# A joint-network training step: gelu's k·x·x as one ScalarE square with a scale, in place of a product and a multiplication on VectorE

## The chip, the cores and the metric

The kernel runs on one core of a Trainium2 chip. The metric is the device time of one execution in microseconds (us), as the median of several runs. The engines are named as the profile names them: PE is TensorE (its weight loads are PEld), DVE is VectorE, ACT is ScalarE, POOL is GpSimd, and SP is SyncE, which here only issues transfers. Every engine works through its own queue strictly in order, and waits on semaphores for the others.

## What is computed

The kernel computes a forward pass and all its gradients. Two convolutions of three taps over time, each followed by gelu and by a halving of the time axis, feed a joint network with eight labels `u`:

```python
h = gelu(conv3(x, w1))[:, ::2]            # x: 2 x 16000 x 256, bf16
f = gelu(conv3(h, w2))[:, ::2]            # f: 2 x 4000 x 256
j = tanh((f @ w_f)[:, :, None] + (g @ w_g)[:, None])   # 2 x 4000 x 8 x 256
out = j @ w_o                             # 2 x 4000 x 8 x 256
# returned: out and the gradients of x, w1, w2, g, w_f, w_g, w_o for grad_out
```

Here gelu is the approximate one, which the kernel writes with a sigmoid: with `k = 0.044715` and `a = 2·sqrt(2/pi)`, `gelu(x) = x·s`, where `s = sigmoid(a·x·(1 + k·x·x))`. The backward pass needs gelu's derivative, `s + a·(1 + 3k·x·x)·(1 - s)·gelu(x)`, and so uses `k·x·x` a second time.

## The kernel before

**Tiling.** Channels lie on the 128 partitions, in two halves (`KT = 2`). Time is cut into 16 chunks, eight for each batch entry, of 512 positions of the quarter-rate axis (`CW`, 416 in the last chunk of a batch entry). A tile of gelu is therefore 128 partitions by 2 x 512 = 1024 elements in bf16. Each chunk has three gelus: two after the first convolution (its even and its odd outputs, `conv_units`) and one after the second (`conv2_units`). In chunk 0 each gelu is cut into two halves of 128x512.

**One gelu** (the function `gelu`, helper lines that the profile puts under L194, or L288 in chunk 0's second convolution). ACT has copied the convolution's result from PSUM to `g_x` (L247, L283). The list `first` computes `g_sq = k·x·x` in two DVE instructions (a product, then a multiplication by a constant), then `g_s = (g_sq + 1)·x` on DVE, then the sigmoid on ACT, in place on `g_s`, and then the product `h = s·x` (written to `HT` or `FT`) on DVE. The list `second` is five more DVE instructions, which turn `g_sq`, `g_s` and `h` into the derivative, written to `G1` or `G2`. They go on using `g_sq`.

**The joint stage.** Over the eight labels of a chunk, `tanh` makes `JT` on ACT (L313) from `FE`; `gj` squares it on ACT (`JSQ`, L524), multiplies `grad_out` by `w_o` on PE (L530), and a DVE instruction combines both to `NGZ` (L532). POOL adds the eight `NGZ` up (`ACCN`, `NGFE`, L551). PE computes `out` (L624), which ACT copies out of PSUM to `OUT` (L626), and the gradient of `w_o` (L673), for which `JR`, a transposed `JT`, is fetched by transposing transfers on SP's queue (chunk 0 does it by PE and DVE instead).

**The backward stage** of the chunk before: `d1_units` (PE L337, DVE `GF` L339), `d5_units` (PE L367, DVE `GH` L370), `gwf_units` and `gw2_units` (PE transposes L381, copied out of PSUM at L383 to `rows` by DVE or ACT, then PE L407 and L438), `e_units` (PE L479, which ACT copies to `GX` at L482, and PE L501). Sums over chunks are added into `ACC` tiles by DVE (L323).

**Order.** The function `weave` runs one chunk's joint stage and fills in, at a set ratio, the convolutions of the next chunk and the backward stage of the chunk before. Gelu's instructions are put on a list `later`, from which `pump` takes two at each step. On top of this a scheduler reorders the instructions of each engine when the program is built, so that the queues' final order is its work, and an instruction more or less can move others.

**PSUM.** Seven buffers of the pool `psp` are shared by all these stages. A PE group that needs a buffer waits until DVE or ACT has read an earlier group out of it.

Of the kernel before, what the change touches and what calls it, by code (L numbers as in the profile page):

```python
# [15 lines left out]
ALU = mybir.AluOpType  # L16
ACT = mybir.ActivationFunctionType

GELU_K = 0.044715
GELU_A = float(2.0 * np.sqrt(2.0 / np.pi))  # L20

P = 128
KT = 2
# [8 lines left out]
def kernel(  # L32
# [22 lines left out]
    nc = tc.nc  # L55
# [127 lines left out]
    def scratch(name, spare):  # L183
        if spare:
            return rowp.tile([P, 8, P], BF16, name="rows")[:].rearrange("p (k a) b -> p k (a b)", k=KT)
        return gel.tile([P, KT, CW], BF16, name=name)
# [9 lines left out]
    def gelu(xb, W, h, gp, off, kts=((0, KT),), spare=False):  # L196

        sq, s = scratch("g_sq", spare), scratch("g_s", spare)
        TT, TS, STT = nc.vector.tensor_tensor, nc.vector.tensor_scalar, nc.vector.scalar_tensor_tensor
        first, second = [], []  # L200
        for (k0, k1) in kts:
            sq_, s_, x_ = sq[:, k0:k1, :W], s[:, k0:k1, :W], xb[:, k0:k1, :W]
            h_, gp_ = h[:, k0:k1, off:off + W], gp[:, k0:k1, off:off + W]
            first += [
                partial(TT, out=sq_, in0=x_, in1=x_, op=ALU.mult),
                partial(TS, out=sq_, in0=sq_, scalar1=GELU_K, scalar2=None, op0=ALU.mult),
                partial(STT, out=s_, in0=sq_, scalar=1.0, in1=x_, op0=ALU.add, op1=ALU.mult),
                partial(nc.scalar.activation, out=s_, in_=s_, func=ACT.Sigmoid, scale=GELU_A),
                partial(TT, out=h_, in0=s_, in1=x_, op=ALU.mult),
            ]  # L210
            second += [
                partial(TS, out=sq_, in0=sq_, scalar1=3.0 * GELU_A, scalar2=GELU_A, op0=ALU.mult, op1=ALU.add),
                partial(TS, out=x_, in0=s_, scalar1=-1.0, scalar2=1.0, op0=ALU.mult, op1=ALU.add),
                partial(TT, out=sq_, in0=sq_, in1=x_, op=ALU.mult),
                partial(TT, out=sq_, in0=sq_, in1=h_, op=ALU.mult),
                partial(TT, out=gp_, in0=sq_, in1=s_, op=ALU.add),
            ]
        return first, second
# [6 lines left out]
    def conv_units(n):  # L225
# [11 lines left out]
        for par in range(2):  # L237
            xb = gel.tile([P, KT, CW], BF16, name="g_x")
            for mt in range(KT):
                ps = ps_f32()  # L240
                k = 0
                for (i, c, sh) in taps[par]:
                    for kt in range(KT):
                        nc.tensor.matmul(ps[:, :W], lhsT=W1[:, i, kt, mt * P:(mt + 1) * P],  # L244
                                         rhs=st["X", c][:, kt, 16 + sh:16 + sh + W], start=(k == 0), stop=(k == 5))
                        k += 1
                nc.scalar.copy(out=xb[:, mt, :W], in_=ps[:, :W])  # L247
                yield
            first, second = gelu(xb, W, HT[:, par], G1[:, par], 2, HALVES if n == 0 else ((0, KT),))
            later.extend(first)  # L250
            seconds += second
            if n == 0:
                pump(len(first))
# [11 lines left out]
    def conv2_units(n):  # L265
        b, ci, c0, W = geom(n)
        st = S[n]
        HT = st["HT"]
        if n > 0:
            pump(len(later))  # L270
        FT = ftp.tile([P, KT, CW], BF16, name="FT")
        G2 = ftp.tile([P, KT, CW], BF16, name="G2")
        st["FT"], st["G2"] = FT, G2
        xb = scratch("g_x", n == 0)
        for mt in range(KT):
            ps = ps_f32()
            k = 0
            for (i, par, off) in ((1, 0, 2), (0, 1, 1), (2, 1, 2)):
                for kt in range(KT):
                    nc.tensor.matmul(ps[:, :W], lhsT=W2[:, i, kt, mt * P:(mt + 1) * P],  # L280
                                     rhs=HT[:, par, kt, off:off + W], start=(k == 0), stop=(k == 5))
                    k += 1
            nc.scalar.copy(out=xb[:, mt, :W], in_=ps[:, :W])  # L283
            yield
        first, second = gelu(xb, W, FT, G2, 0, HALVES if n == 0 else ((0, KT),), n == 0)
        if n == 0:
            for f in first:
                f()  # L288
            seconds0[:0] = second
            later.extend(seconds0)  # L290
        else:
            later.extend(first + second)
# [529 lines left out]
    for i in range(KK):  # L822
# [15 lines left out]
                            in_=NGGEc[:].rearrange("p b k u c -> p (b k u) c"),  # L838
# [53 lines left out]
```

## Time and profile before

| what | value |
|---|---|
| median of 3 runs | 883.72 us (882.99 to 883.83) |
| the profiled execution: its own time | 882.75 us |
| the profiled execution: its span | 881.0 us |
| busy share of the span: PE, DVE, ACT, POOL | 95%, 77%, 73%, 48% |
| mean granted PE clock | 0.993 of full speed |
| one full chunk in the steady part | 52.69 us |

The profile is of one execution. A busy PE is not PE at its peak, because the modelled end of a matmul includes its way through the pipeline; matmuls that follow each other without a gap start at shorter distances than they last. "Idle before, and its releaser" is the time that an engine stood still before an instruction, and the last instruction that it waited for. Most of the span is a repetition of chunks; the first 80 us hold the start, in which nothing of a backward stage exists yet, and the last 80 us hold no gelu.

### The profile page before, as it was taken

The numbers are of one execution on the slowest core, as the hardware profiler recorded it, in microseconds if no ns is written. First come the engines' busy times: TensorE is split into PE (matmuls) and PEld (weight loads), VectorE is DVE, ScalarE is ACT, GpSimd is POOL, SyncE is SP. The second block draws the span as 40 slices with busy tenths as digits, with TensorE's granted clock in tenths as the row PEclk, the third lists the DMA queues.
The fourth block names the chain that finished last, engine by engine and source line by source line (L and its number), as shares of the span: only waits on it lengthen the run. The fifth ranks groups of instructions, "written<-read, shape, count | busy, mean of one in ns | idle before, by whom it ended". The sixth has DMA issues, their size and how long they took to land.

```text
span 881.0 us, 17824 instructions
## 1 busy us (share of the span) xinstructions
PE 833.0 (95%) x6574; PEld 600.6 (68%) x6648; DVE 678.9 (77%) x1296; ACT 639.0 (73%) x1016; POOL 419.6 (48%) x457
## 2 busy tenths in 40 slices
PE   7968999999999999998999999999999999999997
PEld 3545676767768577776756668676776757778875
DVE  5998959869596895959789596986959779596553
ACT  2767797686958769595786958768695876958534
POOL 1254544535535455553554544454554535554651
PEclk9998999999999999999999999999999999999999
DMA  9987999999999999999999999999999999997942
GB/s 207 183 182 164 191 229 233 219 210 231 239 227 229 239 179 258 196 227 214 183 197 201 250 219 224 246 230 250 198 227 225 222 237 194 229 209 175 225 136 94
DMA packets 382456, 185.67 MB, mean 211 GB/s; under 512 B 330160, under 2 KB 366280, under 8 KB 382368
## 3 DMA queue, kind: packets, MB, share of 16 engines
q1 hardware_dynamic: 362400, 114.35, 74.3%
q0 software_dynamic: 19968, 70.18, 26.9%
q8 instruction: 52, 0.85, 0.4%
q14 instruction: 36, 0.29, 0.1%
HBM read 54.43 MB, written 50.34 MB: 119 GB/s over the span
## 4 chain that ended last, share of the span: by engine, by line
PE 42%; DVE 29%; ACT 20%; issue 5%; DMA 2%; POOL 0%; ACTq 0%; POOLq 0%; DVEq 0%
DVE g_sq L194 10%; ACT JT L313 8%; PE GWO_ps L673 6%; PE ps L479 5%; PE ps L501 5%; PE ps L624 5%; DVE g_s L194 4%; PE ps L530 4%; PE ps L438 4%; PE ps L280 4%; PE pst L381 3%; DVE NGZ L532 3%; ACT GX L482 3%; DVE GH L370 3%; ACT JSQ L524 3%
## 5 line engine op out<-in xcount | busy, mean ns | idle before, releaser
L551 POOL TENSOR_TENSOR ACCN<-ACCN,NGZ 128x1024 f32<-128x1024 f32 (+1 forms) x80 | 180.3, 2254 | 174.5 <-DVE NGZ L532 173.3
L532 DVE SCALAR_TENSOR_TENSOR NGZ<-JSQ,ps 128x512 bf16<-128x512 bf16 (+1 forms) x256 | 164.2, 668 | 85.6 <-ACT GX L482 40.6
L524 ACT ACTIVATE JSQ<-JT 128x1024 bf16<-128x1024 bf16 (+1 forms) x128 | 135.3, 1059 | 76.2 <-DVE NGZ L532 76.2
L313 ACT ACTIVATE JT<-FE,GE 128x512 bf16<-128x512 f32 (+1 forms) x256 | 171.2, 738 | 0.1
L624 PE MATMUL ps<-WO,JT 128*128 128x256 bf16 x992 | 147.7, 273 | 5.7 <-DVE NGZ L532 4.9
L626 ACT CAST OUT<-ps 128x512 bf16<-128x512 f32 x248 | 143.4, 605 | 5.1 <-PE ps L624 4.7
L530 PE MATMUL ps<-GOT,WOT 128*128 128x512 bf16 (+1 forms) x472 | 134.2, 373 | 9.4 <-DVE GH L370 7.6
L673 PE MATMUL GWO_ps<-GO,JR 128*128 128x256 bf16 x992 | 139.0, 273 | 0.0
L194 ACT ACTIVATE g_s<-g_s 128x1024 bf16<-128x1024 bf16 (+2 forms) x49 | 49.3, 1005 | 98.0 <-DVE g_s L194 98.0
L624 PEld LDWEIGHTS <-JT 128*128 128x128 bf16 x992 | 94.6, 98 | 31.1 <-issue 9.5
L673 PEld LDWEIGHTS <-JR 128*128 128x128 bf16 x992 | 95.0, 98 | 23.8 <-issue 8.5
L323 DVE TENSOR_TENSOR ACC<-ACC,ps 128x512 f32<-128x512 f32 x90 | 59.2, 680 | 59.9 <-PE ps L501 55.3
L479 PE MATMUL ps<-W1T,GH 128*128 128x256 bf16 (+2 forms) x768 | 104.2, 273 | 0.4 <-ACT g_x L283 0.4
L501 PE MATMUL ps<-rows,X 128*128 128x256 bf16 (+2 forms) x768 | 92.3, 273 | 0.0
L244 PE MATMUL ps<-XC,W 128*128 128x512 bf16 (+1 forms) x370 | 88.6, 374 | 0.7 <-DMA XC<-in_x_dram 0.5
L482 ACT CAST GX<-ps 128x512 bf16<-128x512 f32 (+2 forms) x128 | 76.5, 598 | 14.1 <-PE ps L479 7.4
L479 PEld LDWEIGHTS <-GH 128*128 128x128 bf16 (+2 forms) x768 | 75.0, 99 | 15.9 <-issue 1.8
L501 PEld LDWEIGHTS <-X 128*128 128x128 bf16 (+2 forms) x768 | 74.6, 98 | 12.9 <-issue 1.3
L530 PEld LDWEIGHTS <-WOT 128*128 128x128 bf16 x512 | 49.0, 98 | 48.3 <-issue 9.5
L491 POOL DMA_DIRECT2D out_dram<-GX x64 | 35.7, 558 | 88.8 <-ACT GX L482 84.6
L653 POOL DMA_DIRECT2D out_dram<-OUT x64 | 49.4, 773 | 59.8 <-ACT OUT L626 54.7
L383 ACT COPY rows<-pst 128x1024 bf16<-128x1024 bf16 x64 | 64.2, 1013 | 10.7 <-PE pst L381 10.7
(135 smaller groups left out, 1324.0 us busy)
## 6 DMA issues: line engine op xcount, KB each, us to landing
GO<-in_grad_out_dram SPq DMA_DIRECT2D x56, 512.0 KB, 5.2
out_dram<-OUT POOLq DMA_DIRECT2D x56, 512.0 KB, 5.6
X<-in_x_dram POOLq DMA_DIRECT2D x58, 320.0 KB, 8.0
out_dram<-GX POOLq DMA_DIRECT2D x58, 256.0 KB, 3.8
JR<-JT SPq DMA_TRANSPOSE x240, 4.8
GO<-in_grad_out_dram SPq DMA_DIRECT2D x8, 384.0 KB, 4.0
out_dram<-OUT POOLq DMA_DIRECT2D x8, 384.0 KB, 4.9
GOT<-in_grad_out_dram SPq DMA_TRANSPOSE x128, 5.0
```

The source lines that it names most:

```text
L194: later.popleft()()
L313: nc.scalar.activation(out=JT[:, mt, :W], in_=S[n]["FE"][:, mt, :W], func=ACT.Tanh, bias=GE[:, b, mt, u:u + 1], scale=1.0)
L479: nc.tensor.matmul(ps[:Mx, cj * D:(cj + 1) * D], lhsT=GH[:, par, kt, j:j + Mx], rhs=W1T[:, i, kt, :], start=(k == 0), stop=(k == last))
L482: nc.scalar.copy(out=t[:Mx, 2 * cp:2 * cp + 2, :], in_=ps[:Mx, :])
L501: nc.tensor.matmul(ps[:, dt * D:(dt + 1) * D], lhsT=st["X5", o][:M, i + 2 * par, dt * P:(dt + 1) * P], rhs=t[:M, j + 2 * par:j + 2 * par + ...
L524: nc.scalar.activation(out=JSQ[:, :, :W], in_=JT[:, :, :W], func=ACT.Square)
L530: nc.tensor.matmul(ps[:, :W], lhsT=WOT[:, kt, mt * P:(mt + 1) * P], rhs=GOT[:, kt, :W], start=(kt == 0), stop=(kt == KT - 1))
L532: nc.vector.scalar_tensor_tensor(out=NGZ[:, mt, :W], in0=JSQ[:, mt, :W], scalar=1.0, in1=ps[:, :W], op0=ALU.subtract, op1=ALU.mult, accum_ ...
L551: nc.gpsimd.tensor_tensor(out=out, in0=in0, in1=st["NGZ", u][:, :, :W], op=ALU.add)
L624: nc.tensor.matmul(ps[:M, j * V:(j + 1) * V], lhsT=st["JT", u][:, kt, o:o + M], rhs=WO[:, kt, :], start=(kt == 0), stop=(kt == KT - 1))
L626: nc.scalar.copy(out=OUT[:M, k, :], in_=ps[:M, :])
L673: nc.tensor.matmul(GWO_ps[:, dt, :], lhsT=JR[:M, k, j, dt, :], rhs=GO[:M, k, j * V:(j + 1) * V], start=(n_gwo[0] == 0), stop=(n_gwo[0] == ...
```

## The change

In `gelu`, the two DVE instructions that make `g_sq` (the product `x·x`, and the multiplication by `k`) are replaced by one ACT instruction, the activation Square with `scale = sqrt(k)`, which gives `(sqrt(k)·x)·(sqrt(k)·x)`. It is made 51 times: three times in each of 15 chunks, and six times on halves in chunk 0. All that follows in gelu is as before, and no transfer, buffer or size changes.

```diff
 GELU_A = float(2.0 * np.sqrt(2.0 / np.pi))
+ROOT_K = float(np.sqrt(GELU_K))
...
             first += [
-                partial(TT, out=sq_, in0=x_, in1=x_, op=ALU.mult),
-                partial(TS, out=sq_, in0=sq_, scalar1=GELU_K, scalar2=None, op0=ALU.mult),
+                partial(nc.scalar.activation, out=sq_, in_=x_, func=ACT.Square, scale=ROOT_K),
                 partial(STT, out=s_, in0=sq_, scalar=1.0, in1=x_, op0=ALU.add, op1=ALU.mult),
                 partial(nc.scalar.activation, out=s_, in_=s_, func=ACT.Sigmoid, scale=GELU_A),
                 partial(TT, out=h_, in0=s_, in1=x_, op=ALU.mult),
```

## The prediction

> **What bounds the kernel now.** I read the page's busy shares first, then the steady part cut into pieces of 5 us.
>
> ```profile
> PE 833.0 (95%) x6574; PEld 600.6 (68%) x6648; DVE 678.9 (77%) x1296; ACT 639.0 (73%) x1016; POOL 419.6 (48%) x457
> 26.40:79.10 52.70, 40.92 (x274) 25.44 (x277) 49.46 (x102) 39.27 (x61) 24.00 (x18) 0.94 0.78 167
> 606.98:659.67 52.69, 51.17 (x405) 37.16 (x408) 41.53 (x77) 40.03 (x64) 25.89 (x27) 1.00 1.12 224
> 615.00:620.00 5.00, 3.93 (x26) 2.05 (x26) 5.00 (x11) 2.02 (x3) 0.00 (x1) 1.00 1.10 261
> 650.00:655.00 5.00, 4.95 (x41) 3.81 (x40) 1.23 (x4) 5.00 (x10) 0.71 (x2) 1.00 1.34 200
> ```
>
> Columns of the stretches: PE, PEld, DVE, ACT, POOL busy, clock, DMA. PE is the bound almost everywhere, but 77% for DVE is a mean of two states. At 615 DVE is full and ACT 40% busy; at 650 ACT is full and DVE a quarter. At the start (26 to 79) DVE is 94% busy, and PE stands still for 11.8 us. Next, what PE waits for in one steady chunk (606.9 to 659.6), and the DVE instructions behind it:
>
> ```profile
> PE ps L530 <- DVE GH L370: 0.6, 1, 0.6
> PE ps L367 <- DVE rows L383: 0.2, 1, 0.2
> PE ps L624 <- DVE NGZ L532: 0.2, 1, 0.2
> PE pst L381 <- DVE GH L370: 0.2, 1, 0.2
> ```
>
> ```profile
> 606.98 1.84 DVE L194 TENSOR_TENSOR g_sq<-g_x 128x1024 bf16<-128x1024 bf16 x1 [0.39 <-ACT g_x L247]
> 608.86 0.43 DVE L194 TENSOR_SCALAR g_sq<-g_sq 128x1024 bf16<-128x1024 bf16 x1
> 609.32 1.23 DVE L194 SCALAR_TENSOR_TENSOR g_s<-g_sq,g_x 128x1024 bf16<-128x1024 bf16 x1
> 610.46 0.68 DVE L339 SCALAR_TENSOR_TENSOR GF<-G,ps 128x512 bf16<-128x512 bf16 x1
> ...
> 613.46 0.69 DVE L194 TENSOR_TENSOR g_sq<-g_x 128x1024 bf16<-128x1024 bf16 x1
> ...
> 614.67 0.42 DVE L194 TENSOR_SCALAR g_sq<-g_sq 128x1024 bf16<-128x1024 bf16 x1
> ...
> 617.33 0.68 DVE L383 COPY rows<-pst 128x1024 bf16<-128x1024 bf16 x1
> ```
>
> All of PE's steady waits lie between 610 and 622 and are for DVE emptying PSUM. Counting lost PE start times (a 128x512 matmul follows the last after 0.217 us, six in 1.30; a 128x256 after 0.109, sixteen in 1.75) gives 0.23 at 611.2, 0.81 at 617.47, 0.38 at 618.07, 0.35 at 619.29, 0.18 at 619.90 and 0.32 at 621.10: 2.27 us of a 52.69 us chunk. The chain of waits runs through DVE from 606.98 to 621.06, through both removed pairs. No steady wait of PE is for DMA. One is for ACT, before L438 for its copies to `rows`: eight matmuls in 1.11 us there and in 1.04 elsewhere, so 0.07.
>
> **What goes.** 51 pairs on DVE. Undisturbed, a 128x1024 pair lasts 0.69 + 0.42 and moves the queue on by 0.60 + 0.33 = 0.93 us; three per chunk are 2.8 us. Many take longer: the product's 39 full tiles average 1166 ns, and the one at 606.98 took 1.84 while POOL's L551 ran from 606.15 to 608.27. That excess need not vanish: the next such DVE instruction can meet the same POOL instruction.
>
> **What comes.** 51 squares on ACT. The nearest row is `JSQ`, the same operation on the same shape: 1080 ns, some 0.96 of queue time. With 45 full-width ones and six halves (sigmoid on half a tile: 0.63) that is 39 x 1.08 + 6 x 0.91 + 6 x 0.63 = 51 us, taking ACT from 639 to 690 us, 78%. A function table to load is excluded: the trace has one load, 1.28 us at 0.74, and tanh, Square and sigmoid alternate after it.
>
> The Trainium skill speaks against the change: "ScalarE: Activation LUTs", section "Rules for kernel authors", says to use VectorE for a multiplication, up to about three times faster per element in bf16. This trace has 0.42 against 1.08 for the scalar multiplication, but two instructions go for one, 1.11 against 1.08. By that rule alone a third of 1.08 in place of it would make the move lose 0.7 us per gelu. "Perfetto Trace Analysis", section "Optimizing Scalar/DVE Operations", allows it where DVE is saturated, which the rows at 615 show.
>
> **Where they land, and the new wait.** The changed kernel's queues keep PE's steady order nearly whole; DVE's GH and `rows` swap a place here and there. On ACT, each square takes the place of a `JSQ` or stands behind one `OUT` copy, and the `JSQ` follows. DVE's `g_s` now waits for ACT; behind it in DVE's queue stand `GF`, GH and `rows`, and PE waits for those. I walk this stretch with the durations above.
>
> First gelu: the square takes the slot of the `JSQ` at 607.88, ends near 608.95, and `g_s` starts at 608.97 instead of 609.32. DVE idles over 2 us, but the second `GF` comes 0.35 earlier, and PE's 0.23 at 611.2 goes. The sigmoid, now behind a `JSQ`, comes 0.23 later, and so does `HT`. Then the second pair is gone: the first GH starts at 613.69 (before 614.07). Its square, behind one `OUT` copy, ends near 613.85, in time for `g_s` at 614.30 (before 615.60). Second GH 616.03 (616.73), `HT` 616.64 (617.94), second `rows` 617.25 (617.33), `NGZ` 617.85 (618.55), third GH 620.0 (620.37). So PE's L530 comes 0.70 earlier, but L367 behind it still needs the second `rows`: 0.09. The last of these waits, L381 on the third GH, ends 0.37 earlier; that is what the chunk keeps. Of the 2.27 us most stay, because `rows` hardly moves. On ACT a `JSQ` goes behind the fourth `rows` copy, which should free the 0.07 before L438. The postponed `JSQ` is harmless: in the walk it ends at 611, and its `NGZ` starts at 617.85. Bounds: nothing (a later `rows` takes it all) to 1.0 us (a second wait falls too); I take 0.44, the walk and the 0.07. Third gelu: `g_s` comes some 2 us earlier (its multiplication took 1.75 at 635.1), but PE does not wait for `FT` there: nothing. 14 such chunks (52.69 us windows from 80.08 to 817.74): **6.2 us**. No transfer is moved past a square there: `JR` waits for tanh, and the tanh keep their places before the square.
>
> **The start.** Up to 29 us, DVE's chain of half-tile gelus shortens, and by the same kind of walk the first L303 is ready some 2.5 us earlier. But L244 at 31.81 waits for a transposed x that SP's queue issues in its own time; that caps the gain near 0.4, the DVE work brought forward aside. From 26 to 79 PE waits for DVE:
>
> ```profile
> 46.81 0.60 PE L624 MATMUL ps<-WO,JT 128*128 128x256 bf16 x4 [2.60 <-DVE NGZ L532]
> 50.30 0.38 PE L280 MATMUL ps<-HT,W 128*128 128x512 bf16 x1 [1.37 <-DVE JR L383]
> 69.46 1.01 PE L303 MATMUL ps<-FT,WF 128*128 128x512 bf16 x2 [5.37 <-DVE FT L194]
> 70.26 1.91 PE L381 MATMUL pst<-ident,JT 128*128 128x128 bf16 x16
> ```
>
> Three pairs go there: 2.8 us undisturbed; with the two that were held up (2.29 for a product, 2.30 for a multiplication) 6.3. The wait of 5.37 is also followed by slow matmuls (sixteen transposes in 1.91, 1.06 elsewhere), some 2 us that a shorter wait could spare. ACT is 75% busy here and adds 3.2 us, one sigmoid now behind four tanh. I take 4, between 1 and 9, near the undisturbed price because a held-up place passes to its successor. With the 0.4: **4.4 us**. The last 80 us hold no gelu: nothing.
>
> **Sum.** 882.75 (the profiled execution) - 6.2 - 4.4 = 872.15. The median stands 0.97 above that execution: **873 us**.
>
> **Rivals.**
> - *ACT becomes the late one (slower).* In 14 chunks the first square stands in a queue that has been full since 589. If it starts more than 0.35 us later than 607.88 (one more `OUT` copy is 0.6 of queue, a `JSQ` 0.96), `g_s` is later than before and `GF`, GH and `rows` with it: 0.3 to 0.6 a chunk, 4 to 8 us, with a start that gains 1 or 2 at most: 885.5 to 891. For it: DVE is then idle at 607 to 609, with everything behind it. Against: two removed instructions still lie in the chain after it, worth 0.9. Chance 0.11.
> - *Absorbed.* The second `rows` and third GH come no earlier, since the queues are built around the same PE order, and only the start gains or loses: 0 to 5 us, 878 to 885. The walk's 0.08 at `rows` speaks for it. Chance 0.16.
> - *More than forecast.* `rows` moves ahead of the wait and the held-up start goes in full: 14 x 1.0 + 9 = 23, down to 861, or a little under; 866 and less. DVE's 2 us of freedom per chunk speak for it. Chance 0.13.
> - *Forecast*, 866 to 878: 0.60.
>
> **Chances.** What a measurement here can tell from no change is about 0.2%, 1.8 us: 882.0 to 885.5. Faster takes the forecast, the larger gain and half of the absorbed case: 0.81. The other half is no change: 0.08. Slower: 0.11. The range runs from 861, leaving out 0.05 below, to 883, leaving out the slower case and some of the absorbed one.
>
> **What would show it.** Right: DVE busy near 600 us and ACT near 690; a steady chunk of 52.0 to 52.4; the wait of PE's L530 for GH gone or under 0.2, that of L367 for `rows` grown towards 1; PE idle from 26 to 79 down from 11.8 to about 8; `g_s` on DVE waiting for ACT. Wrong: a chunk of 52.7 or more; ACT named as the one that PE's L367 or L381 waits for, through a late `g_s`; or a stall for `FT` at 69 as long as before.

## The result, and the profile after

The changed kernel takes 868.86 us as the median of 4 runs (868.64 to 869.8), against 883.36 us before (882.48 to 883.83): a ratio of 0.9841, 95% interval 0.9822 to 0.9859. The forecast was 873 us, range 861 to 883, with 0.81 on faster. The sign and the mechanism were right, and the gain was some 4 us larger than forecast. The profiled execution took 868.84 us, its span is 867.1 us, and the readings of the changed kernel below are from it. Of all the executions below one (e10's, 879.34 us, where its others took 861 to 865) fell in a slower state of the chip; the ratios leave it out.

First the busy shares, and the two stretches that answer to those of before: the start, and one steady chunk (columns as before).

```profile
PE 832.6 (96%) x6648; PEld 600.7 (69%) x6648; DVE 610.6 (70%) x1194; ACT 686.9 (79%) x1067; POOL 411.5 (47%) x457
```

```profile
26.40:79.10 52.70, 42.99 (x294) 26.52 (x292) 41.96 (x92) 45.09 (x71) 25.89 (x21) 0.97 0.89 194
590.65:642.89 52.24, 51.24 (x410) 37.26 (x409) 37.35 (x70) 43.10 (x67) 25.15 (x26) 1.00 1.08 228
```

DVE has 102 instructions fewer and ACT 51 more. The steady chunk went from 52.69 to 52.24 us. In the stretch from 26 to 79 PE now stands still for 52.70 - 42.99 = 9.7 us (11.8 before).

The waits of PE in that chunk (us in total, times, longest), and, among those of DVE, the one for the square:

```profile
PE ps L367 <- DVE rows L383: 0.6, 1, 0.6
PE pst L381 <- DVE GH L370: 0.3, 1, 0.3
```

```profile
DVE g_s L195 <- ACT g_sq L195: 3.0, 2, 2.4
```

The wait of L530 for GH is gone, and the one behind it, L367 for `rows`, grew: what the prediction called "L367 behind it still needs the second `rows`". The new wait of DVE for ACT is 3.0 us a chunk, longer than any wait of PE, and costs PE nothing here, because the DVE queue had that time to spare.

Of DVE's instructions in the same stretch, those of the walk:

```profile
595.05 0.68 DVE L339 SCALAR_TENSOR_TENSOR GF<-G,ps 128x512 bf16<-128x512 bf16 x1
598.17 1.23 DVE L195 SCALAR_TENSOR_TENSOR g_s<-g_sq,g_x 128x1024 bf16<-128x1024 bf16 x1 [2.44 <-ACT g_sq L195]
599.32 0.68 DVE L339 SCALAR_TENSOR_TENSOR GF<-G,ps 128x512 bf16<-128x512 bf16 x1
602.84 0.68 DVE L370 TENSOR_TENSOR GH<-ps,G 128x512 bf16<-128x512 f32 x1
603.44 1.21 DVE L195 SCALAR_TENSOR_TENSOR g_s<-g_sq,g_x 128x1024 bf16<-128x1024 bf16 x1
605.17 0.68 DVE L370 TENSOR_TENSOR GH<-ps,G 128x512 bf16<-128x512 f32 x1
606.38 0.68 DVE L383 COPY rows<-pst 128x1024 bf16<-128x1024 bf16 x1
606.98 0.68 DVE L532 SCALAR_TENSOR_TENSOR NGZ<-JSQ,ps 128x512 bf16<-128x512 bf16 x1
609.13 0.69 DVE L370 TENSOR_TENSOR GH<-ps,G 128x512 bf16<-128x512 f32 x1
```

This chunk begins 10.86 us earlier on its clock than the one of before. With that added, the walk's times and the measured ones are: first `g_s` 608.97 and 609.03, first GH 613.69 and 613.70, second `g_s` 614.30 and 614.30, second GH 616.03 and 616.03, second `rows` 617.25 and 617.24, `NGZ` 617.85 and 617.84, third GH 620.0 and 619.99. The second `GF` came at 610.18, so 0.28 earlier than before, where the walk had 0.35.

**Where the 13.9 us of span went.** The first `GF` (L339) of each chunk marks the chunks. Before, the first mark lies at 80.65 and the last at 851.1; after, at 76.13 and 837.2. So the start gave 4.5, the chunks 9.4, and the end nothing. The chunks' lengths:

| intervals between marks | before | after | gain of each |
|---|---|---|---|
| 3, 4, 10 to 13: regular | 52.68 to 52.69, the last 52.20 | 52.24 to 52.25, the last 51.76 | 0.43 to 0.44 |
| 2 | 52.72 | 52.09 | 0.63 |
| 5, 6, 7, 9, 14: uneven, around the ends of a batch entry | 52.89, 51.27, 50.78, 52.70, 48.72 | 51.78, 50.02, 49.56, 51.39, 46.99 | 1.1 to 1.7, in all 6.6 |
| 1 and 8: after the start, and across the batch entries | 52.64, 54.22 | 53.12, 54.24 | -0.48, -0.02 |

The forecast's 0.44 for a regular chunk is exact. The surprise is in the uneven chunks, which gain three times as much.

### The profile page after: what moved, and what is told of

Same layout as the page of the kernel before. It is cut to its first block, busy times and chain, and to the rows that moved or that the text cites. A ratio compares the mean times of both kernels' runs of the same rounds, so it can differ in the third digit from the quotient of the medians.

```text
span 867.1 us, 17795 instructions
## 1 busy us (share of the span) xinstructions
PE 832.6 (96%) x6648; PEld 600.7 (69%) x6648; DVE 610.6 (70%) x1194; ACT 686.9 (79%) x1067; POOL 411.5 (47%) x457
## 3 DMA queue, kind: packets, MB, share of 16 engines
q1 hardware_dynamic: 362400, 114.35, 75.8%
## 4 chain that ended last, share of the span: by engine, by line
PE 49%; ACT 28%; DVE 14%; issue 6%; DMA 3%; POOL 0%; ACTq 0%; DVEq 0%; POOLq 0%
ACT JT L313 11%; PE GWO_ps L673 7%; PE ps L624 6%; PE ps L479 5%; PE ps L501 5%; PE ps L438 5%; PE ps L530 5%; PE pst L381 4%; PE ps L280 4%; ACT JSQ L524 4%; ACT OUT L626 3%; ACT GX L482 3%; DVE g_sq L195 3%; DVE g_s L195 3%; DVE GH L370 2%
## 5 line engine op out<-in xcount | busy, mean ns | idle before, releaser
L551 POOL TENSOR_TENSOR ACCN<-ACCN,NGZ 128x1024 f32<-128x1024 f32 (+1 forms) x80 | 173.1, 2163 | 150.4 <-DVE NGZ L532 149.1
L532 DVE SCALAR_TENSOR_TENSOR NGZ<-JSQ,ps 128x512 bf16<-128x512 bf16 (+1 forms) x256 | 166.5, 670 | 96.0 <-PE ps L530 47.3
L626 ACT CAST OUT<-ps 128x512 bf16<-128x512 f32 x248 | 149.5, 611 | 9.1 <-PE ps L624 9.0
L624 PE MATMUL ps<-WO,JT 128*128 128x256 bf16 x992 | 148.0, 273 | 1.3 <-DVE NGZ L532 0.9
L530 PE MATMUL ps<-GOT,WOT 128*128 128x512 bf16 (+1 forms) x512 | 138.5, 374 | 2.1 <-DVE JR L383 2.1
L624 PEld LDWEIGHTS <-JT 128*128 128x128 bf16 x992 | 94.8, 98 | 25.9 <-issue 2.4
L195 DVE SCALAR_TENSOR_TENSOR g_s<-g_sq,g_x 128x1024 bf16<-128x1024 bf16 (+2 forms) x49 | 78.0, 1591 | 42.7 <-ACT g_sq L195 42.6
L244 PE MATMUL ps<-XC,W 128*128 128x512 bf16 (+1 forms) x384 | 91.8, 376 | 3.3 <-DMA XC<-in_x_dram 3.0
L653 POOL DMA_DIRECT2D out_dram<-OUT x64 | 49.4, 773 | 83.4 <-ACT OUT L626 78.6
L482 ACT CAST GX<-ps 128x512 bf16<-128x512 f32 (+2 forms) x128 | 74.2, 591 | 15.5 <-PE ps L479 8.2
L530 PEld LDWEIGHTS <-WOT 128*128 128x128 bf16 x512 | 48.9, 98 | 42.4 <-issue 3.0
L491 POOL DMA_DIRECT2D out_dram<-GX x64 | 35.7, 558 | 87.6 <-ACT GX L482 80.9
L383 ACT COPY rows<-pst 128x1024 bf16<-128x1024 bf16 x64 | 63.9, 1026 | 15.5 <-PE pst L381 15.5
```

What stands on the lines that cost most here:

```text
L195: later.popleft()()
L482: nc.scalar.copy(out=t[:Mx, 2 * cp:2 * cp + 2, :], in_=ps[:Mx, :])
L530: nc.tensor.matmul(ps[:, :W], lhsT=WOT[:, kt, mt * P:(mt + 1) * P], rhs=GOT[:, kt, :W], start=(kt == 0), stop=(kt == KT - 1))
L532: nc.vector.scalar_tensor_tensor(out=NGZ[:, mt, :W], in0=JSQ[:, mt, :W], scalar=1.0, in1=ps[:, :W], op0=ALU.subtract, op1=ALU.mult, accum_ ...
L551: nc.gpsimd.tensor_tensor(out=out, in0=in0, in1=st["NGZ", u][:, :, :W], op=ALU.add)
L624: nc.tensor.matmul(ps[:M, j * V:(j + 1) * V], lhsT=st["JT", u][:, kt, o:o + M], rhs=WO[:, kt, :], start=(kt == 0), stop=(kt == KT - 1))
```

## The experiments

The main theory is that *place* decides: an instruction taken from DVE is worth what the PE wait behind it is worth, nearly all of it in the second gelu. The rival is that DVE's *load* decides, so that each third of the move is worth about a third of the gain. A third possibility, that only the order into which the scheduler puts the queues pays, is not told apart by any run: no kernel here keeps the queues' order and changes the instructions alone, so place always means the place that the scheduler gives. The edit that most runs share gives `gelu` a switch:

```diff
-    def gelu(xb, W, h, gp, off, kts=((0, KT),), spare=False):
+    def gelu(xb, W, h, gp, off, kts=((0, KT),), spare=False, act=True):
...
+            if act:
+                first.append(partial(nc.scalar.activation, out=sq_, in_=x_, func=ACT.Square, scale=ROOT_K))
+            else:
+                first += [
+                    partial(TT, out=sq_, in0=x_, in1=x_, op=ALU.mult),
+                    partial(TS, out=sq_, in0=sq_, scalar1=GELU_K, scalar2=None, op0=ALU.mult),
+                ]
             first += [
-                partial(nc.scalar.activation, out=sq_, in_=x_, func=ACT.Square, scale=ROOT_K),
...
```

It adds six lines, so in those kernels L367 is L373, L381 is L387, L530 is L536 and L339 is L345. Ratios are to the kernel before on the same chip, with their 95% intervals; "first mark" is the first `GF`.

| run | squares on ACT | median, us | ratio | first mark | regular chunk |
|---|---|---|---|---|---|
| before | none | 883.36 | 1 | 80.65 | 52.69 |
| after | all | 868.86 | 0.9841 [0.9822, 0.9859] | 76.1 | 52.24 |
| e1 | all, in chunks 0 and 1 only | 879.57 | 0.9949 [0.993, 0.9968] | 75.8 | 52.69 |
| e2 | all, from chunk 2 on | 875.25 | 0.9909 [0.9884, 0.9934] | 81.4 | 52.25 |
| e3 | second gelu | 875.07 | 0.9907 [0.9877, 0.9938] | 75.8 | 52.22 |
| e4 | third gelu | 880.26 | 0.9958 [0.9941, 0.9974] | 76.7 | 52.74 |
| e5 | first gelu | 879.66 | 0.9945 [0.9925, 0.9964] | 80.9 | 52.64 |
| e6 | all, each square made twice | 878.0 | 0.9932 [0.9906, 0.9958] | 78.6 | 52.53 |
| e7 | none; one DVE instruction for the pair | 887.15 | 1.0033 [1.0018, 1.0047] | 83.2 | 52.70 |
| e8 | all; both L383 copies of `gwf_units` on ACT too | 872.04 | 0.9858 [0.9833, 0.9883] | 77.8 | 52.16 |
| e9 | all (the changed kernel again) | 870.61 | 0.9869 [0.9835, 0.9903] | 75.8 | 52.24 |
| e10 | all; the first L383 copy of `gwf_units` on ACT too | 864.66 | 0.9782 [0.9759, 0.9805] | 73.6 | 51.85 |
| e11 | all in chunks 0 and 1, then first and second | 872.29 | 0.9887 [0.9864, 0.9909] | 73.7 | 52.51 |
| e12 | all in chunks 0 and 1, then second and third | 873.44 | 0.9879 [0.985, 0.9908] | 75.7 | 52.21 |

The changed kernel stands in the table twice, with ratios of 0.9841 and 0.9869 whose intervals overlap. Differences of that size between two rows (e8, e11 and e12 against it) therefore show nothing by themselves. The lengths of its regular chunks agree within 0.02 between the two profiles, and the readings below go by lengths and waits, each from one profiled execution.

**The start against the steady part (e1, e2).** `act=n <= 1` and `act=n >= 2`.

> The square is on ACT in the gelus of chunks 0 and 1 alone; chunks 2 to 15 keep the pair on DVE. Theory 1, place decides (only DVE work ahead of a PSUM read that PE waits for pays): the traces before and after show the first GF of the chunk at 80 us 4.5 us earlier, so 4.5 us less than before, 878 to 880 us, and steady chunks of 52.69. Theory 2, load decides (DVE busy time saved pays wherever it lies): 12 of 51 squares, six of them halves, so some 9 of 48 full ones, a fifth of 14.5 us, 880.5 us. Theory 3, only the new order of the queues pays: not told apart here.

> The other half: the pair stays on DVE in chunks 0 and 1, the square is on ACT from chunk 2 on. Theory 1: the steady part alone gives 9 to 10 us, 873 to 875 us, with chunks of 52.25 in the middle, and together with the run on the start the gains add up to the whole 14.5. Theory 2: four fifths of 14.5, 872 us. If the gain of a steady chunk came from the start (queues further ahead), it would be 878 or more.

Measured against 883.71: 4.1 us and 8.5 us less. Each half shows only in its own part: e1's first mark is 75.8 and its regular chunk 52.69, e2's are 81.4 and 52.25, with the uneven chunks as in the full change (51.79, 50.04, 49.57, 51.40). The two halves add up to 12.6 of the 14.5 us, where e2's expectation had the whole. In e2's profile the first mark is 0.8 later than before, and one chunk (53.57, with a wait of 1.1 for `GF`) is 1.3 longer than in the full change, which is about what is missing.

**One gelu at a time (e3, e4, e5).** `act` is true for `par == 1`, for the second convolution, or for `par == 0`.

> Only the second gelu of each chunk (odd outputs of the first convolution) has its square on ACT. Theory 1: a walk through the queues as before gives GH 0.6 earlier, the second rows 0.3 later, the third GH 0.57 earlier, so PE 0.5 us per chunk; 14 x 0.5 and some 1 to 2 us at the start, 873 to 876 us. Theory 2: a third of 14.5, 878.5 us.

> Only the third gelu of each chunk (second convolution) has its square on ACT. Theory 1: nothing in the steady chunks (52.6 to 52.7), since PE doesn't wait for FT there, and 2 to 3 us at the start, where L303 waits for FT: 880 to 882 us. Theory 2: a third of 14.5, 878.5 us. Theory 4, the pairs' being held up by POOL is what pays (this gelu's multiplication took 1.75 us in each steady chunk): more than a third, 876 us or less.

> Only the first gelu of each chunk (even outputs of the first convolution) has its square on ACT. Theory 1: the second GF comes 0.35 earlier but the sigmoid behind the square and a JSQ 0.23 later, so that GH, rows and the third GH come 0.2 later: 14 x 0.2 us lost, 1 to 2 us won at the start, 883 to 886 us. Theory 2: a third of 14.5, 878.5 us.

One chunk of e3's profiled run lasted 57.92 us, with PE waiting 3.5 us for a transfer to `JR`; 52.22 is the length of the regular chunks beside it. The second gelu alone makes the whole regular gain (52.22), and the third and the first make none of it (52.74, 52.64). That is place, not load. In the start the second and the third each bring the first mark to about 76, and together to no less: their gains overlap, so the three runs' gains (8.6, 3.5 and 4.3 us) do not add up. e5 missed its expectation of a loss: its regular chunks stand still (one chunk near the start is 0.7 longer), and its uneven ones gain 0.7 to 0.9, the last 1.4. For one uneven chunk (interval 5) the waits of PE show why. First before (291.4 to 344.3), then with the first gelu's square alone on ACT (e5, 292 to 344.1); waits of 0.2 are left out:

```profile
PE ps L367 <- DVE GF L339: 0.8, 1, 0.8
PE ps L530 <- DVE GH L370: 0.6, 1, 0.6
```

```profile
PE ps L536 <- DVE GH L376: 1.0, 1, 1.0
```

In this chunk PE waits 0.8 for the second `GF`, which stands behind the first gelu's pair and its `g_s`. The pair's product is held up longer than in a regular chunk (2.52 against 1.84). With the square on ACT `g_s` comes earlier, and the wait for `GF` goes. DVE before, then in e5:

```profile
292.45 2.52 DVE L194 TENSOR_TENSOR g_sq<-g_x 128x1024 bf16<-128x1024 bf16 x1 [0.40 <-ACT g_x L247]
295.46 1.23 DVE L194 SCALAR_TENSOR_TENSOR g_s<-g_sq,g_x 128x1024 bf16<-128x1024 bf16 x1
```

```profile
295.10 1.23 DVE L195 SCALAR_TENSOR_TENSOR g_s<-g_sq,g_x 128x1024 bf16<-128x1024 bf16 x1 [2.46 <-ACT g_sq L195]
```

Counted from the chunk's mark (291.37 and 291.96), `g_s` starts at 4.09 before and at 3.14 in e5. In a regular chunk it moves only from 3.40 to 3.13, no wait for `GF` stands behind it, and bringing it earlier is worth nothing.

**A slower square (e6).** The activation is issued twice in a row.

```diff
                 partial(nc.scalar.activation, out=sq_, in_=x_, func=ACT.Square, scale=ROOT_K),
+                partial(nc.scalar.activation, out=sq_, in_=x_, func=ACT.Square, scale=ROOT_K),
```

> As the changed kernel, but every square on ACT is made twice, the second over the first with the same result. Theory 1: the first square of a chunk has only 0.35 us of slack; a second one is 0.96 us of ACT's queue, so g_s, GF, GH and rows come later by up to 0.9 a chunk: 868.9 + 12 and some 2 at the start, 880 to 886 us, with DVE's g_s waiting for ACT over 3 us in each chunk. Rival, ACT has room (79% busy would become 85%): 868.9 to 871 us.

It gives back some 8 or 9 of the 14.5 us: a regular chunk loses 0.29, and the first mark comes 2.4 later. The expected 880 to 886 were too high. They went by the changed kernel's order, but here the scheduler put the second `GF` ahead of the late `g_s`. DVE, one steady chunk of this kernel:

```profile
657.01 0.69 DVE L340 SCALAR_TENSOR_TENSOR GF<-G,ps 128x512 bf16<-128x512 bf16 x1 [1.73 <-PE ps L338]
659.63 1.23 DVE L195 SCALAR_TENSOR_TENSOR g_s<-g_sq,g_x 128x1024 bf16<-128x1024 bf16 x1 [1.94 <-ACT g_sq L195]
```

So the cover over the new wait is thin, as the slower rival said, and one square more uses it up. That the other order of the DVE queue took a part of the price back is read from these rows, and was not tested apart.

**Fewer DVE instructions, on DVE (e7).** The pair as one instruction, `(x·k)·x`.

```diff
-                partial(nc.scalar.activation, out=sq_, in_=x_, func=ACT.Square, scale=ROOT_K),
+                partial(STT, out=sq_, in0=x_, scalar=GELU_K, in1=x_, op0=ALU.mult, op1=ALU.mult),
```

> The pair becomes one DVE instruction, (x*k)*x, and nothing goes to ACT. It is of the kind of g_s, 1.22 us (1.13 of queue) where the undisturbed pair takes 0.93. Theory 1: two of them in the chain of each chunk, 14 x 0.4 us and the start, 886 to 892 us, a little less where the pair was held up by POOL. Rival, fewer instructions pay wherever they run: below 883 us.

It is 0.33% slower than before. An undisturbed instruction of this form lasts 1.22 us on a 128x1024 tile, the pair 0.69 + 0.42 = 1.11, and in the queue the pair moves on by 0.93. Regular chunks did not lose the 0.4 expected (52.70). Their first pair was held up before, and the one instruction is held up too: from its start to that of `g_s` pass 2.39 us, against 2.34. The second one moves the queue on by 1.13 instead of 0.93, and why the chunk does not feel it stays open. The profiled execution's loss of 5.6 lies mostly in the first mark (2.6 later), the interval behind it (1.7) and the one across the batch entries (1.8); a clock reading further below explains part of it.

**What is left (e8, e10, with e9 as the yardstick).** L367 now waits for the second `rows`. So both copies to `rows` in `gwf_units` were moved to ACT (e8), and then only the first (e10).

```diff
-            transposes(srcs, dsts)
+            transposes(srcs, dsts, nc.scalar.copy)
```

```diff
-            transposes(srcs, dsts)
+            transposes(srcs, dsts, nc.scalar.copy if k == 0 else None)
```

> As the changed kernel, and the two copies to rows of the gwf stage (L383, 0.60 us of DVE's queue each) are made by ACT, which stands still for over 3 us in this stretch. In the changed kernel PE's L367 waits 0.62 us for the second of them in each steady chunk, and L381 0.34 us for the third GH. Theory 1: rows ends near 606.7 instead of 607.06, both waits shrink, 0.4 to 0.7 us per chunk, 858 to 864 us. Rival, PE waits for the next thing (ACT late with rows for gw2, or GF): 867 us or more.

> The changed kernel itself, as the yardstick for the other two of this group. All theories: 868 to 870 us, first backward stage (the first GF) near 76, regular chunk 52.24.

> The changed kernel, with only the first of the two copies to rows of the gradient of w_f (k = 0) moved from DVE to ACT. Theory 'what is left of the steady wait is the place of the second rows copy on DVE': DVE reaches the second copy some 0.6 us earlier and ACT's own rows for the gradient of w2 are not yet due, so a regular chunk goes from 52.24 to 51.8 to 52.0, in all 863 to 867 us. Rival 'the wait moves to ACT, as when both copies were moved': PE's L367 or L438 waits for ACT's rows, regular chunk 52.15 or more, uneven chunks longer, 869 to 873 us.

With both copies on ACT the wait only changes its cause. PE's waits in a regular chunk of e8:

```profile
PE ps L367 <- ACT rows L383: 0.4, 1, 0.4
PE ps L438 <- ACT rows L383: 0.3, 1, 0.3
PE ps L530 <- DVE GH L370: 0.2, 1, 0.2
```

A chunk gains 0.08, two uneven ones lose 1.4 and 1.5, and the whole is no faster than the changed kernel (ratio 0.9858 against 0.9841 and 0.9869): the rival of that expectation. With one copy moved, a regular chunk is 51.85 and the median 864.66 us, the best of the kernels here (ratio 0.9782 against 0.9869 for the changed kernel in the same group, the intervals apart). Its DVE and its PE in a regular chunk:

```profile
588.62 0.68 DVE L339 SCALAR_TENSOR_TENSOR GF<-G,ps 128x512 bf16<-128x512 bf16 x1
599.96 0.68 DVE L383 COPY rows<-pst 128x1024 bf16<-128x1024 bf16 x1
602.11 0.68 DVE L370 TENSOR_TENSOR GH<-ps,G 128x512 bf16<-128x512 f32 x1
```

```profile
599.48 0.38 PE L530 MATMUL ps<-GOT,WOT 128*128 128x512 bf16 x1 [0.19 <-DVE GH L370]
600.70 1.03 PE L367 MATMUL ps<-GF,W2T 128*128 128x512 bf16 x4 [0.84 <-DVE rows L383]
```

The number was as expected, the reason only in part. Counted from `GF`, `rows` comes at 599.96 - 588.62 = 11.34, and in the changed kernel at 606.38 - 595.05 = 11.33: the scheduler filled the free place ahead of it with one of gelu's later products. The third GH comes at 13.49 instead of 14.08, and L381's wait for it (0.3) is no longer listed, so the chunk's gain runs through the third GH and not through `rows`. The two medians lie 6 us apart. A part of that is likely the start, whose first mark is 2.2 earlier than in e9's profile, of which more under the clock below.

**Do the three gelus depend on each other? (e11, e12).** From chunk 2 on, the third (e11) or the first (e12) gelu has its pair back on DVE.

> The changed kernel, with the product and the multiplication back on DVE in the third gelu (second convolution) from chunk 2 on; start, first and second gelu as changed. Theory 'place decides, and the third gelu has none in the steady part': regular chunk 52.2 to 52.3, uneven chunks within 0.2 of the changed kernel, in all 867.5 to 871 us. Rival 'DVE's load counts wherever it lies': a third of the steady gain is lost, some 3 us, 871 to 874 us.

> The changed kernel, with the product and the multiplication back on DVE in the first gelu from chunk 2 on; start, second and third gelu as changed. It completes the table of which gelu is on ACT in the steady part. So far a regular chunk: none 52.69, first 52.64, second 52.22, third 52.74, first and second 52.51, all three 52.24. Theory 'with the first square on ACT, DVE's first g_s hangs on ACT's full stretch, and this costs what first and second showed (0.29); without it the second's gain is kept': regular chunk 51.9 to 52.25, uneven chunks up to 0.5 longer than the changed kernel, in all 867 to 872 us. Rival 'the first pair on DVE pushes the second gelu's g_s later by its 0.35, whatever else': regular chunk 52.4 to 52.6, 872 to 876 us.

The expectation for e11 missed, 52.51 instead of 52.2 to 52.3, and this is where "the third gelu: nothing" holds only with a condition. With the second square on ACT throughout, the regular chunks of four runs are:

| | third pair on DVE | third square on ACT |
|---|---|---|
| first pair on DVE | 52.22 (e3) | 52.21 (e12) |
| first square on ACT | 52.51 (e11) | 52.24 (after) |

The third gelu is worth 0.27, but only if the first is on ACT. The trace suggests how. In e11 ACT waits 2.59 us before the third sigmoid for the pair on DVE, whose product is held up (2.44); in the changed kernel it waits 0.49. From that sigmoid until the next chunk's first square ACT hardly pauses. So the square comes later, and with it DVE's first `g_s`. ACT's sigmoid and DVE's `g_s` in e11:

```profile
628.51 1.06 ACT L195 ACTIVATE g_s<-g_s 128x1024 bf16<-128x1024 bf16 x1 [2.59 <-DVE g_s L195]
```

```profile
599.39 1.23 DVE L195 SCALAR_TENSOR_TENSOR g_s<-g_sq,g_x 128x1024 bf16<-128x1024 bf16 x1 [2.71 <-ACT g_sq L195]
```

In e11 `g_s` starts 3.40 after the chunk's first `GF` (595.99), in the changed kernel 3.12: 0.28 later, and the chunk is 0.27 longer. This is the prediction's slower rival ("ACT becomes the late one"), in a kernel that moves only two of the three. The table shows the dependence; that it runs through ACT's full stretch is read from the trace and was not tested apart.

e12's regular chunks are as expected (52.21); its uneven ones are longer by up to 0.9, where 0.5 was allowed, and the 873.44 us lie above the 867 to 872. The lost wait is back, in the chunk that runs from 285.6 to 338.1:

```profile
PE ps L373 <- DVE GF L345: 0.8, 1, 0.8
PE ps L373 <- DVE rows L389: 0.6, 1, 0.6
```

The wait for `GF` does not explain every uneven chunk. Before the change it is listed in intervals 5, 6 and 14 (0.8, 0.7 and 1.2). In 7 and 9 PE waits for a GH instead (1.2 at L381, 0.7 at L530), and in e12's interval 6 a wait of 0.4 for `GF` is back while the chunk is only 0.1 longer. What the five share is the start of the first `g_s`, counted from the chunk's mark:

| first `g_s` after the mark, us | regular | 5 | 6 | 7 | 9 | 14 |
|---|---|---|---|---|---|---|
| before | 3.40 | 4.09 | 3.72 | 3.03 | 3.40 | 4.20 |
| e5, first square alone on ACT | 3.13 | 3.14 | 2.21 | 1.37 | 2.26 | 2.20 |
| after | 3.12 | 3.13 | 2.19 | 1.35 | 2.26 | 2.19 |
| e12, first pair back on DVE | 3.40 | 4.08 | 3.40 | 3.04 | 3.41 | 4.20 |

So the first gelu's share lies in the uneven chunks, where its square brings `g_s` 1.0 to 2.0 earlier instead of 0.3. That is shown from both sides, since e5 has it and e12 loses it. Which wait of PE it shortens differs from chunk to chunk.

## Why the prediction was right, and which step was mis-sized

- **The regular chunk (0.44).** Right in size (0.43 to 0.44) and, within 0.1 us, in each step of the walk. Both of its terms came: the third GH is 0.38 earlier, and the eight matmuls of L438 take 1.04 instead of 1.11. That all of it is the second gelu's was shown by e3, e4 and e5.
- **The mis-sized term: 14 x 0.44 = 6.2.** The intervals gave 9.4. The prediction took every chunk for the steady one it had read. In five of them the first square brings `g_s` 1.0 to 2.0 earlier, and these gained 6.6 instead of 5 x 0.44 = 2.2. Two intervals gained nothing, which the 14 had not allowed for either: in them the first `g_s` starts later than before (4.35 and 3.34 after the mark, for 3.40 and 2.49) and waits for the square. The view of PE's waits before, cut by chunk, shows other waits than the steady ones in four of the five (`GF` in 5, 6 and 14, a GH of 1.2 in 7); only one chunk had been cut.
- **The start (4.4).** Measured 4.5, but in other parts, so the agreement of the sum is partly luck. The first L303 is ready 2.3 us earlier (25.18 for 27.48), and the prediction said that L244's transposed x would cap that near 0.4. The cap took all of it, since L244 starts at 31.77 instead of 31.81; PE now waits there itself, and pays for it with its clock (below), which the prediction had not foreseen; this is also why PE's idle time from 26 to 79 is 9.7 and not about 8. The wait for `FT` fell from 5.37 to 1.84, and the slow matmuls behind it went: sixteen transposes take 1.06 instead of 1.91.

```profile
31.77 0.59 PE L244 MATMUL ps<-XC,W 128*128 128x512 bf16 x2 [2.97 <-DMA XC<-in_x_dram]
64.49 0.59 PE L303 MATMUL ps<-FT,WF 128*128 128x512 bf16 x2 [1.84 <-DVE FT L195]
```

- **"A held-up place passes to its successor."** Right, and larger than thought. The row of `g_s` after:

```profile
L195 DVE SCALAR_TENSOR_TENSOR g_s<-g_sq,g_x 128x1024 bf16<-128x1024 bf16 (+2 forms) x49 | 78.0, 1591 | 42.7 <-ACT g_sq L195 42.6
```

  It was 56.4 us, 1152 ns on the mean. So 21.6 us of busy time came back in an instruction that nobody changed, which is part of why DVE stands at 610.6 and not near 600.
- **"Third gelu: nothing."** Right for the third alone (e4), wrong beside the first (e11): 0.27 a chunk.
- **The rivals.** "More than forecast" was half right: the gain was larger, though not because `rows` moved. "Absorbed" fell with the walk. "ACT becomes the late one" did not decide here, but the lower end of the price that it named (0.3 to 0.6 a chunk) is near what e6 and e11 measured (0.29 and 0.27).

## What to carry to other kernels

Cost a moved instruction by the wait of the bounding engine that stands behind it, and cut that view for every kind of chunk, not for one steady chunk: the chunks at the ends of a batch may wait for something else. When the replacement makes a second engine wait, look for where that engine's full stretch begins: in e11 a square 0.2 to 0.3 us later at the end of such a stretch went with a chunk 0.27 longer. When one wait is gone, move as little as the next one needs: one copy more on ACT gained 0.4 a chunk, two gained 0.08.

## What the hardware showed that was not expected

**A wait of 2 to 3 us can cost PE its clock.** The stretches behind L244's wait in the changed kernel (2.97 us, 28.80 to 31.77), and in e10, where the same transfer landed earlier and PE waited 1.74:

```profile
30.00:32.00 2.00, 0.23 (x2) 0.11 (x2) 0.42 (x1) 1.23 (x2) 0.39 (x2) 1.00 1.03 208
32.00:34.00 2.00, 1.79 (x17) 1.37 (x16) 1.38 (x4) 1.60 (x3) 0.00 (x0) 0.65 0.88 144
34.00:36.00 2.00, 2.00 (x10) 1.07 (x9) 2.00 (x8) 0.83 (x2) 0.44 (x1) 0.50 0.41 77
```

```profile
30.63 0.59 PE L244 MATMUL ps<-XC,W 128*128 128x512 bf16 x2 [1.74 <-DMA XC<-in_x_dram]
```

```profile
32.00:34.00 2.00, 1.95 (x17) 1.36 (x18) 2.00 (x7) 1.69 (x3) 0.00 (x0) 1.00 0.35 64
34.00:36.00 2.00, 2.00 (x15) 1.30 (x14) 1.34 (x5) 1.66 (x4) 1.58 (x1) 1.00 0.74 150
```

The granted clock (the third number from the end) falls to half until 36, which by an estimate from these rows costs 2 x 0.35 + 2 x 0.50 = 1.7 us; with the shorter wait it stays at 1.00. From 24 us on, single waits of up to 1.90 us were not followed by half clock in any profile here, though three close together were (3.5 us in all, e3). All from 2.74 on were. In between the length does not decide: it fell after 2.09 (e2), 2.10 (e11), 2.35 and 2.43 (e9) and 2.45 (e7), but not after 2.60 in the kernel before (L624 at 46.81), 2.41 (e7), or 2.12 and 2.67 (e6). What decides there is not shown. So a transfer that lands a little earlier or later can move a run by some 2 us, and a part of e10's lead over e9, whose profile shows half clock after 2.35 at L244 and after 2.43 between the batch entries, is likely of this kind. The Trainium skill, "TensorE: Matmul & The Clock Gate", section "Why this matters for your kernels", warns of idle gaps above about 3 us; here some of 2.1 were enough.

**DVE's `g_s` and the product stand still while POOL adds.** POOL's two instructions and DVE's `g_s` in e9, at the change of batch entries:

```profile
440.85 2.13 POOL L551 TENSOR_TENSOR ACCN<-NGZ 128x1024 f32<-128x1024 bf16 x1
442.91 1.21 POOL L358 COPY GH<-GHh 128x2 bf16<-128x2 bf16 x1
```

```profile
440.54 3.53 DVE L195 SCALAR_TENSOR_TENSOR g_s<-g_sq,g_x 128x1024 bf16<-128x1024 bf16 x1 [2.77 <-ACT g_sq L195]
444.00 0.57 DVE L339 SCALAR_TENSOR_TENSOR GF<-G,ps 128x416 bf16<-128x416 bf16 x1
```

`g_s` takes 1.2 us undisturbed. Here it ends 1.09 after POOL's addition (L551, until 442.98), so it does nearly all of its work behind it. The other full-width ones that L551 held up in the changed kernel's steady part end 1.07 to 1.09 after it, and before the change the held-up products (0.69 undisturbed) ended 0.54 to 0.56 after it. Not every DVE instruction is held up: an `NGZ` and a copy to `rows`, which read PSUM, take their usual 0.69 at 621.41 and 622.03 in the changed kernel, while L551 runs from 620.20 to 624.53. POOL's small copy (L358) takes 0.19 in other chunks; here it stands behind `g_s` in its turn, and takes 1.21. In the profile of the changed kernel the addition had started 1.65 earlier (439.20), and `g_s` took 1.90. Behind it stands `GF`, for which PE then waited 2.43 instead of 0.80. The Trainium skill, "SBUF — State Buffer", section "SBUF: two separate sides", tells of a port pair that VectorE and GpSimd lock against each other, where the loser fully blocks. These rows agree with the blocking; which lock it was, and why `g_s` lost to an addition whose row begins 0.31 later, no run here shows.
